# A Fourier mix and channel-mix kernel: the first two key pieces ordered by feature half, slots 4 to 7 mixed in four operations, one evacuation moved ahead of two

## The chip, the core and the metric

The kernel runs on one core of a Trainium2 chip. A core has a matrix engine (PE, with its weight loads shown apart as PEld), a vector engine (DVE), a scalar engine (ACT), a general engine (POOL) and a queue engine (SP). Each takes its own instructions in the order in which they were written, and engines wait for one another through semaphores. The metric is the time of one execution on the device in microseconds (us), lower is better; the median of several runs stands for a kernel.

## What is computed

For `x` of shape (8, 3072, 256): a two-dimensional Fourier transform per batch element, of which the real part is kept, and then a channel mix with a shift by one position.

```python
X = np.fft.fft(np.fft.fft(x, axis=1), axis=2).real       # (8, 3072, 256)
x_prev = X shifted by one position, zeros first
xk = mu_k * X + (1 - mu_k) * x_prev
xr = mu_r * X + (1 - mu_r) * x_prev
k = np.maximum(xk @ w_k, 0)                              # 256 -> 1024
v = (k * k) @ w_v                                        # 1024 -> 256
out = sigmoid(xr @ w_r) * v
```

`w_k` is (256, 1024), `w_v` (1024, 256), `w_r` (256, 256). The output is float32; inside, the kernel works in 16-bit floats with 32-bit sums.

## The kernel before

**Layout.** The transform is done as matmuls with tables of sines and cosines that the kernel builds at its start. Its result for a batch element is the tile `y` (in `y_t[b]`): 128 partitions hold features, the free axis holds slots of 64 positions, and in each slot the two feature halves `a = 0, 1` (features 0 to 127 and 128 to 255). Half of the sequence is covered by some 26 slots, and the other half is read from the mirrored ones. The mixed input `x` (`x_t[b, j, m]`; j = 0 for the key, 1 for the gate, m = 0 or 1 for the half of the sequence) has 24 slots for each feature half, that is 2 by 1536 columns.

**Mixing.** `diff` forms `d`, the difference of neighbouring slots, in one vector operation. `mix_part` then forms `x = y + mu * d` for a range of slots in one of two ways. For `j` = 0 and `lo` up to 4 it does one fused operation for each feature half (L738: multiply by a per-partition scalar, then add, in one instruction). Otherwise it does four operations: `scaled` for both halves (L711, a multiplication into the tile `t`), then `mixed` for both halves (L722, an addition). `mix_part` is called for the slots 4 to 7 and 8 to 15 of the first key input; the slots 0 to 3 have code of their own (L887 on ACT, then four fused operations on DVE, L892, two for each feature half), which takes them from PSUM.

**Key products.** The positions are worked in 48 chunks of 512 (`chunks`, each `(b, m, i)`), and each chunk in four K pieces (`ds` = 0 to 3). A piece gives 256 of the 1024 columns of `xk @ w_k` in a PSUM tile of 1024 columns from the three slots of `ps_w`. `k_products` (L749 to L760) issues its matmuls: two blocks of 128 columns (`hs`), and for each the two feature halves `a` = 0 and 1, which add up in PSUM; each matmul has a weight load of its own. `k_piece` issues the products, then the ReLU on ACT (L767). `square` squares the result on DVE (L777), or in a few steps on ACT (L775). `v_part` (L804) multiplies the squares by `w_v` in the first chunks, one piece at a time, three steps behind (`SHORT`); `v_tile` does so later on, a block of 128 positions at a time. `v_out` multiplies by the gate and sends the result out.

**Order.** The order of the instructions on every engine is the order in which the code issues them, which `pin_order` fixes at the end. The main loop runs over steps, one K piece each, and other work is hung on steps with `at` and `event`. Only the first chunk is special: its pieces 0 and 1 are done in two parts. The products for its first 256 positions (slots 0 to 3) are issued ahead of the main loop (L948, L949), those for its second 256 positions (slots 4 to 7) at steps 0 and 1.

**Around the change.** Ahead of the main loop the code issues, in this order: the two early products (L948, L949); `diff(0, 4, 8)` and `mix_part(0, 0, 4, 8)` on DVE; `d_small(0, 8, 2)` and `d_small(0, 10, 2)`, each four matmuls (L604) into one of the two PSUM slots of `ps_v` and an evacuation into `g_all` on ACT (L521); `y_evac(0, 0, 4, first)`, an evacuation of four slots of `y` on ACT out of the PSUM tile `first` (L521); then `diff(0, 8, 16)`. At step 0 follow `mix_part(0, 0, 8, 16)` and `diff(0, 0, 4)`, at step 1 one more `d_small`. The PSUM tile of piece 2 is the slot that `first` holds until then, and that of piece 3 is the slot of piece 0.

Of the kernel before, what the change touches and what calls it, by code (L numbers as in the profile page):

```python
# [20 lines left out]
def _v(ap, extra_offset, free_dims):  # L21
    new_ap = [list(ap.ap[0])] + [[s, c] for (s, c) in free_dims]
    return dataclasses.replace(ap, offset=ap.offset + extra_offset, ap=new_ap)
# [16 lines left out]
def kernel(  # L40
# [37 lines left out]
    def ps_w():  # L78
        return ps_slot("W", 3, 1024)

    def ps_v():
        return ps_slot("V", 2, 512)
# [434 lines left out]
    def evac(out_ap, in_ap, eng):  # L517
        if eng == "V":
            V.tensor_copy(out=out_ap, in_=in_ap)
        else:  # L520
            nc.scalar.activation(out=out_ap, in_=in_ap, func=AF.Copy)  # L521
# [75 lines left out]
    def d_units(b, ps, u0, n, bank):  # L597

        for i in range(n):
            for e in range(2):
                o = bank * e + 128 * i
                nc.tensor.matmul(out=ps[:, o:o + 128],  # L604
                                 lhsT=a_t[b][:, e, 2 * (u0 + i):2 * (u0 + i) + 2, :],
                                 rhs=w_eo[:, e], start=True, stop=True)

    def d_evac(ps, u0, n, bank, eng):
        evac(_v(g_all, 256 * u0, [(64, 2), (128, 2 * n), (1, 64)]),
             _v(ps, 0, [(bank, 2), (64, 2 * n), (1, 64)]), eng)  # L610
# [8 lines left out]
    def d_small(b, u, n, eng="A"):  # L619
        ps = ps_v()  # L620
        d_units(b, ps, u, n, 256)
        d_evac(ps, u, n, 256, eng)
# [35 lines left out]
    def y_evac(b, s0, n, ps):  # L658
        o = s0 % 2
        evac(y_t[b][:, s0:s0 + n].rearrange("p s a t -> p (s a t)"),  # L660
             _v(ps, 512 * o, [(128, n // 2), (512 - 1024 * o, 2), (1, 128)]), "A")
# [32 lines left out]
    def diff(b, lo, hi, hs=(0, 1)):  # L694
        if b not in x_t:
            x_t[b] = mix_pool.tile([P, 26, 2, 64], FP16, name="d")
        y = y_t[b]
        a0, a1 = hs[0], hs[-1] + 1
        V.tensor_tensor(out=x_t[b][:, lo:hi, a0:a1], in0=y[:, lo + 1:hi + 1, a0:a1],  # L699
                        in1=y[:, lo:hi, a0:a1], op=ALU.subtract)  # L700

    def scaled(b, j, m, a, lo, hi, eng="V"):

        if a == 0:
            x_t["t", a] = mix_pool.tile([P, 24, 64], FP16, name="t0")
        else:
            x_t["t", a] = mix_pool.tile([P, 24, 64], FP16, name="t1")
        mu = (mu_m if m else mu_f)[:, a, j:j + 1]
        src, dst = x_t[b][:, 2 * m + lo:2 * m + hi, a], x_t["t", a][:, lo:hi]
        if eng == "V":  # L710
            V.tensor_scalar(out=dst, in0=src, scalar1=mu, scalar2=None, op0=ALU.mult)  # L711
        else:
            nc.scalar.activation(out=dst, in_=src, func=AF.Copy, scale=mu)

    def mixed(b, j, m, a, lo, hi):

        if (a, lo) == (0, 0):
            x_t[b, j, m] = mix_pool.tile([P, 2, 1536], FP16, name=f"x{j}{m}")  # L720
        o, step = (1536 * a + 1535 - 64 * lo, -1) if m else (1536 * a + 64 * lo, 1)
        V.tensor_tensor(out=_v(x_t[b, j, m], o, [(64 * step, hi - lo), (step, 64)]),  # L722
                        in0=y_t[b][:, lo + 3 * m:hi + 3 * m, a], in1=x_t["t", a][:, lo:hi],
                        op=ALU.subtract if m else ALU.add)

    def mix_part(b, j, lo, hi):
        if j or lo > 4:
            for a in range(2):
                scaled(b, j, 0, a, lo, hi)
            for a in range(2):  # L730
                mixed(b, j, 0, a, lo, hi)
            return


        if lo == 0:
            x_t[b, j, 0] = mix_pool.tile([P, 2, 1536], FP16, name=f"x{j}0")
        for a in range(2):
            V.scalar_tensor_tensor(out=_v(x_t[b, j, 0], 1536 * a + 64 * lo,  # L738
                                          [(64, hi - lo), (1, 64)]),
                                   in0=x_t[b][:, lo:hi, a], scalar=mu_f[:, a, j:j + 1],  # L740
                                   in1=y_t[b][:, lo:hi, a], op0=ALU.mult, op1=ALU.add)
# [4 lines left out]

    k2_t, st = {}, {}

    def k_products(c, ds, lo=0, hi=512):  # L749
        b, m, i = c  # L750
        xk = x_t[b, 0, m]
        if lo == 0:
            st["k", ds] = ps_w()
        for hs in range(2):
            fc = 2 * ds + hs
            for a in range(2):
                nc.tensor.matmul(out=st["k", ds][:, 512 * hs + lo:512 * hs + hi],  # L757
                                 lhsT=wk_sb[m][a][:, 128 * fc:128 * fc + 128],
                                 rhs=xk[:, a, 512 * i + lo:512 * i + hi],
                                 start=(a == 0), stop=(a == 1))  # L760

    def k_piece(c, ds):
        if ds == 0:
            k2_t[c] = k2_pool.tile([P, 8, 512], FP16, name="k2", tag="k2")
            st["rl"] = k2_pool.tile([P, 8, 512], FP16, name="rl", tag="rl")
        k_products(c, ds, 256 if c == chunks[0] and ds < 2 else 0)
        nc.scalar.activation(out=st["rl"][:, 2 * ds:2 * ds + 2],  # L767
                             in_=st["k", ds].rearrange("p (f t) -> p f t", f=2),
                             func=AF.Relu, bias=0.0, scale=0.25)
# [101 lines left out]
    w, first = ps_w(), ps_w()  # L871
# [56 lines left out]
    chunks = [(b, m, i) for b in range(B) for m in range(2) for i in range(3)]  # L928
# [16 lines left out]
    for n, c in enumerate(chunks[:EARLY]):  # L945
        o_steps[4 * n + SHORT + 3] = [(c, 1, 2), (c, 3, 2)]
    o_steps[4 * EARLY + SHORT + 3] = [(chunks[EARLY], 1, 2)]
    k_products(chunks[0], 0, 0, 256)  # L948
    k_products(chunks[0], 1, 0, 256)  # L949
    diff(0, 4, 8)  # L950
    mix_part(0, 0, 4, 8)
    d_small(0, 8, 2)
    d_small(0, 10, 2)
    y_evac(0, 0, 4, first)
    diff(0, 8, 16)
    at(0, mix_part, 0, 0, 8, 16)
    at(0, diff, 0, 0, 4)
    at(1, d_small, 0, 12, 1)
    at(2, mix_part, 0, 1, 0, 8)
    event(3, (half_tables,))  # L960
    event(4, (c_item, 0, 17, 8))
# [67 lines left out]
    for b in range(B):  # L1029
# [9 lines left out]
        if t < B:  # L1039
# [6 lines left out]
            c = [(c_pairs, t, 8 * n, (8, 8, 8, 4)[n], EV[n]) for n in range(4)]  # L1046
# [21 lines left out]
    for step in range(nk + LAG):  # L1068
        if step < nk:
            k_piece(chunks[step // 4], step % 4)  # L1070
        due(step, "x")
        v = v_steps.get(step)
        if v and step not in early_v:
            v_tile(*v)
        if step in p_steps:
            v_part(*p_steps[step])
        due(step, "e")
        if step + 1 in early_v:
            v_tile(*v_steps[step + 1])
        early = step in OUT_FIRST  # L1080
        for v in o_steps.get(step, ()) if early else ():
            v_out(*v)
        due(step, "w")
        for v in () if early else o_steps.get(step, ()):
            v_out(*v)
        if step < 4 * EARLY + 4:
            square(chunks[step // 4], step % 4, 1, step in SQUARE_A)
        elif step < nk and step % 2:
            square(chunks[step // 4], step % 4)
# [32 lines left out]
```

## Time and profile before

| | |
|---|---|
| median of 3 runs | 431.68 us (431.59 to 433.62) |
| the profiled execution | 431.61 us, of which its span is 429.8 us |
| instructions in the span | 9301 |
| DMA traffic in the span | 42.06 MB, mean 98 GB/s |
| costliest group on PE | L757, the key products: 776 matmuls, 195.7 us busy |
| costliest group on ACT | L767, the ReLU: 192 instructions, 195.2 us busy |
| costliest group on DVE | L777, the squares: 101 instructions, 116.3 us busy |

All times of the profile are counted from the start of the span, and the execution's own time is 1.81 us longer than the span. In a timeline each row gives the start, the busy time, the engine, the line, the operation with output and inputs, the shape and the count; the bracket at the end gives idle time just before and what ended it. Rows of one operation can overlap a little, since an engine starts the next instruction while the last one drains. Ends of matmuls are modelled.

### The profile page before, as it was taken

The page shows a single profiled execution, that of the slowest core. Times are in us where ns is not written, and L with a number is a line of the kernel's source. Part 1 is how long each engine was busy: PE and PEld are TensorE (multiplying, and loading weights), DVE is VectorE, ACT ScalarE, POOL GpSimd, SP SyncE. Part 2 cuts the span into 40 slices and gives each one's busy share as a digit, 9 for nine tenths or more (in the row PEclk, how much of TensorE's full clock was granted, in tenths as well). Part 3 has the DMA queues.
Part 4 walks back from the last instruction along what each step waited for, and adds up shares of the span by engine and source line. Part 5 has one row for each costly group of instructions (what it writes and reads, how often), then busy time and mean ns, then how long its engine had stood idle before and what let it go on. Part 6 is the DMA issues. An engine that isn't in the chain of part 4 may idle for free.

```text
span 429.8 us, 9301 instructions
## 1 busy us (share of the span) xinstructions
PE 422.9 (98%) x3858; PEld 298.0 (69%) x3858; DVE 360.9 (84%) x547; ACT 320.2 (74%) x373; POOL 63.4 (15%) x96
## 2 busy tenths in 40 slices
PE   8999999999999999999999999999999999999996
PEld 3667776777777776776677777777767767766765
DVE  8899989997998889988898988989799847997453
ACT  7889897877878678776777777777786767666661
POOL 7686302000050002300041000500000000000000
PEclk9999999999999999999999999999999999999999
DMA  8999917322286233933269223763232322223233
GB/s 169 134 152 207 231 48 129 76 56 68 71 147 150 51 76 63 191 93 72 58 115 188 57 55 72 135 157 75 53 72 50 76 64 61 70 64 72 67 74 98
DMA packets 35103, 42.06 MB, mean 98 GB/s; under 512 B 4115, under 2 KB 31093, under 8 KB 35061
## 3 DMA queue, kind: packets, MB, share of 16 engines
q1 hardware_dynamic: 27488, 25.41, 23.7%
q0 software_dynamic: 7264, 15.80, 22.5%
q8 instruction: 30, 0.49, 0.5%
q10 hardware_dynamic: 308, 0.26, 0.2%
q14 instruction: 13, 0.10, 0.1%
HBM read 32.08 MB, written 25.17 MB: 133 GB/s over the span
## 4 chain that ended last, share of the span: by engine, by line
PE 94%; ACT 3%; DVE 1%; DMA 1%; issue 0%; ACTq 0%
PE psW L757 39%; PE psV L798 36%; PE psW L784 10%; PE psV L810 3%; PE psW L604 2%; PE psW L678 1%; PE psW L564 1%; DMA mu_row<-in_moe_mu_r_dram 1%; PE psW L646 1%; ACT a L521 1%; ACT m_cs L440 0%; PE psW L582 0%; ACT L839 0%; DVE x L892 0%; ACT rl L396 0%; ACT rl L767 0%
## 5 line engine op out<-in xcount | busy, mean ns | idle before, releaser
L767 ACT ACTIVATE rl<-psW 128x1024 f16<-128x1024 f32 x192 | 195.2, 1025 | 92.5 <-PE psW L757 89.0
L757 PE MATMUL psW<-x,wk 128*128 128x512 f16 (+1 forms) x776 | 195.7, 377 | 0.5
L798 PE MATMUL psV<-wv_sb,k 128*128 128x256 f16 x1424 | 184.1, 273 | 0.0
L798 PEld LDWEIGHTS <-k 128*128 128x128 f16 x1424 | 136.8, 98 | 35.9
L777 DVE TENSOR_TENSOR k<-rl 128x2048 f16<-128x2048 f16 (+1 forms) x101 | 116.3, 1152 | 33.4 <-ACT rl L767 33.0
L757 PEld LDWEIGHTS <-wk 128*128 128x128 f16 x776 | 74.8, 98 | 53.5 <-issue 1.3
L820 DVE SCALAR_TENSOR_TENSOR o<-psV,r 128x512 f32<-128x512 f32 (+1 forms) x97 | 65.8, 681 | 15.1 <-PE psV L798 13.5
L722 DVE TENSOR_TENSOR x<-y,t 128x1536 f16<-128x1536 f16 (+2 forms) x72 | 61.6, 860 | 2.1
L784 PE MATMUL psW<-wr,x 128*128 128x256 f16 x384 | 49.8, 273 | 0.0
L789 ACT ACTIVATE r<-psW 128x1024 f16<-128x1024 f32 x48 | 48.9, 1019 | 0.8 <-PE psW L784 0.8
L784 PEld LDWEIGHTS <-x 128*128 128x128 f16 x384 | 37.4, 98 | 14.4 <-issue 0.2
L463 POOL IOTA gate<- 1x1 int32 x6 | 2.1, 356 | 199.4 <-DVE gate L462 199.4
L521 ACT ACTIVATE a<-psW 128x832 f16<-128x832 f32 x31 | 25.9, 862 | 1.4 <-PE psW L564 1.4
L521 ACT ACTIVATE g_all<-psW 128x1024 f16<-128x1024 f32 (+5 forms) x37 | 25.6, 695 | 0.4 <-PE psW L627 0.2
L140 POOL DMA_INDIRECT xm<-in_x_dram,idx_g x18 | 24.2, 1344 | 5.5 <-issue 5.5
L171 DVE TENSOR_TENSOR p<-xp,xm 112x2304 f16<-112x2304 f16 (+6 forms) x19 | 21.6, 1139 | 0.0
L711 DVE TENSOR_SCALAR t<-d,muf_t 128x1536 f16<-128x1536 f16 (+2 forms) x40 | 20.8, 529 | 0.0
L711 DVE TENSOR_SCALAR t<-d,mu_m 128x1536 f16<-128x1536 f16 x32 | 19.6, 614 | 0.0
L604 PEld LDWEIGHTS <-a 128*128 128x128 f16 x208 | 14.0, 98 | 6.6 <-ACT a L521 0.6
L182 DVE TENSOR_TENSOR eo<-p 112x1152 f16<-112x1152 f16 (+3 forms) x28 | 17.9, 679 | 0.0
L521 ACT ACTIVATE pq<-psW 128x1024 f16<-128x1024 f32 (+1 forms) x18 | 15.2, 879 | 2.3 <-PE psW L678 2.3
L699 DVE TENSOR_TENSOR d<-y 128x1664 f16<-128x1664 f16 (+5 forms) x19 | 16.7, 880 | 0.0
(137 smaller groups left out, 217.7 us busy)
## 6 DMA issues: line engine op xcount, KB each, us to landing
out_dram<-o SPq DMA_DIRECT2D x189, 128.0 KB, 2.4
xp<-in_x_dram POOLq DMA_DIRECT2D x12, 216.0 KB, 4.5
xp<-in_x_dram POOLq DMA_DIRECT2D x13, 192.0 KB, 7.4
xp<-in_x_dram POOLq DMA_DIRECT2D x2, 384.0 KB, 6.9
wv_sb<-in_moe_w_v_dram POOLq DMA_DIRECT2D x1, 512.0 KB, 8.2
xp<-in_x_dram SPq DMA_DIRECT2D x1, 480.0 KB, 4.7
xp<-in_x_dram POOLq DMA_DIRECT2D x1, 432.0 KB, 6.4
xm<-in_x_dram,idx_g POOLq DMA_INDIRECT x18, 7.9
```

The source lines that it names most:

```text
L140: nc.gpsimd.indirect_dma_start(dst, None, src, bass.IndirectOffsetOnAxis(ap=idx, axis=0))
L521: nc.scalar.activation(out=out_ap, in_=in_ap, func=AF.Copy)
L604: nc.tensor.matmul(out=ps[:, o:o + 128], lhsT=a_t[b][:, e, 2 * (u0 + i):2 * (u0 + i) + 2, :], rhs=w_eo[:, e], start=True, stop=True)
L711: V.tensor_scalar(out=dst, in0=src, scalar1=mu, scalar2=None, op0=ALU.mult)
L722: V.tensor_tensor(out=_v(x_t[b, j, m], o, [(64 * step, hi - lo), (step, 64)]), in0=y_t[b][:, lo + 3 * m:hi + 3 * m, a], in1=x_t["t", a][:, ...
L757: nc.tensor.matmul(out=st["k", ds][:, 512 * hs + lo:512 * hs + hi], lhsT=wk_sb[m][a][:, 128 * fc:128 * fc + 128], rhs=xk[:, a, 512 * i + l ...
L767: nc.scalar.activation(out=st["rl"][:, 2 * ds:2 * ds + 2], in_=st["k", ds].rearrange("p (f t) -> p f t", f=2), func=AF.Relu, bias=0.0, sca ...
L777: V.tensor_tensor(out=k2_t[c][:, lo:hi], in0=r, in1=r, op=ALU.mult)
L784: nc.tensor.matmul(out=ps[:, 256 * tb:256 * tb + 256], lhsT=x_t[b, 1, m][:, a, 512 * i + 128 * tb: 512 * i + 128 * tb + 128], rhs=wr_sb[m] ...
L789: nc.scalar.activation(out=st["r", c], in_=ps, func=AF.Sigmoid)
L798: nc.tensor.matmul(out=st["v", tb - h][:, 256 * h:256 * h + 256], lhsT=k2_t[c][:, fc, 128 * tb:128 * tb + 128], rhs=wv_sb[:, fc], start=(f ...
L820: V.scalar_tensor_tensor(out=o.rearrange("p a b -> p (a b)")[:, 0:256 * n], in0=st["v", t0][:, 0:256 * n], scalar=16.0, in1=st["r", c][:, ...
```

## The change

Three things are edited. First, `k_products` takes the feature halves that it is to issue, and a new function, `k_early`, issues the products of pieces 0 and 1 of the first chunk in a given order of (feature half, piece): ahead of the loop first half of the features for both pieces, then the second half for both; in the loop the same, with the last group issued at step 1, behind the ReLU of piece 0 in the code. Second, `mix_part` uses the fused form for slots from 0 on alone, and so slots 4 to 7 of the first key input are mixed in four operations, not two. Third, `y_evac(0, 0, 4, first)` is issued ahead of the two `d_small`.

```diff
     def mix_part(b, j, lo, hi):
-        if j or lo > 4:
+        if j or lo:
             for a in range(2):
                 scaled(b, j, 0, a, lo, hi)
             for a in range(2):
...
-    def k_products(c, ds, lo=0, hi=512):
+    def k_products(c, ds, lo=0, hi=512, halves=(0, 1)):
         b, m, i = c
         xk = x_t[b, 0, m]
-        if lo == 0:
+        if lo == 0 and halves[0] == 0:
             st["k", ds] = ps_w()
         for hs in range(2):
             fc = 2 * ds + hs
-            for a in range(2):
+            for a in halves:
                 nc.tensor.matmul(out=st["k", ds][:, 512 * hs + lo:512 * hs + hi],
...
+    def k_early(lo, hi, which):
+        for a, ds in which:
+            k_products(chunks[0], ds, lo, hi, (a,))
+
     def k_piece(c, ds):
...
-        k_products(c, ds, 256 if c == chunks[0] and ds < 2 else 0)
+        if c == chunks[0] and ds < 2:
+            if ds == 0:
+                k_early(256, 512, ((0, 0), (0, 1), (1, 0)))
+            else:
+                k_early(256, 512, ((1, 1),))
+        else:
+            k_products(c, ds)
         nc.scalar.activation(out=st["rl"][:, 2 * ds:2 * ds + 2],
...
-    k_products(chunks[0], 0, 0, 256)
-    k_products(chunks[0], 1, 0, 256)
+    k_early(0, 256, ((0, 0), (0, 1), (1, 0), (1, 1)))
     diff(0, 4, 8)
     mix_part(0, 0, 4, 8)
+    y_evac(0, 0, 4, first)
     d_small(0, 8, 2)
     d_small(0, 10, 2)
-    y_evac(0, 0, 4, first)
     diff(0, 8, 16)
     at(0, mix_part, 0, 0, 8, 16)
     at(0, diff, 0, 0, 4)
```

## The prediction

> **What bounds the kernel now.** I read the page's span and engines first, then busy time by stretches, then the chain of waits.
>
> ```profile
> span 429.8 us, 9301 instructions
> PE 422.9 (98%) x3858; PEld 298.0 (69%) x3858; DVE 360.9 (84%) x547; ACT 320.2 (74%) x373; POOL 63.4 (15%) x96
> ```
>
> PE is busy for nearly the whole span. The stretches show where it is not; the columns are the stretch, its length, and the busy time and count for each engine, then the granted PE clock and the DMA share.
>
> ```profile
> 8.00:10.00 2.00, 1.44 (x10) 0.68 (x9) 1.97 (x4) 2.00 (x4) 1.68 (x7) 1.00 1.07 201
> 18.00:20.00 2.00, 1.80 (x24) 1.32 (x19) 1.97 (x6) 1.26 (x4) 1.39 (x2) 1.00 1.38 140
> 20.00:22.00 2.00, 1.86 (x13) 1.22 (x13) 1.96 (x6) 2.00 (x4) 1.70 (x2) 1.00 1.02 189
> 22.00:24.00 2.00, 1.99 (x13) 1.00 (x12) 2.00 (x5) 2.00 (x4) 1.62 (x6) 1.00 1.10 180
> ...
> 100.00:200.00 100.00, 100.00 (x934) 70.98 (x927) 88.43 (x114) 75.72 (x83) 12.84 (x16) 1.00 0.47 100
> ```
>
> From 100 to 200 us PE has no hole. The edits all lie between 17 and 24 us, where PE lacks 0.20, 0.14 and 0.01 us in three stretches. So whatever this change does is settled by the moment at which PE starts its unbroken run, and moves the end by as much. The chain of waits (start, length, what) names that moment:
>
> ```profile
> 17.38 1.13 DVE x L892 x4
> ...
> 19.47 0.89 DVE x L738 x2
> ...
> 20.41 0.93 PE psW L757 x7
> ...
> 21.44 1.87 PE psW L757 x8
> ...
> 23.32 1.05 PE psV L810 x8
> ```
>
> The chain runs on DVE to 20.36, through the pair L738 that the change splits, and then on PE. But a chain follows one releaser only. DVE itself, row by row, and the wait for its square:
>
> ```profile
> 18.42 0.68 DVE L519 CAST y<-psV 128x512 f16<-128x512 f32 x1
> 19.02 0.42 DVE L699 TENSOR_TENSOR d<-y 128x512 f16<-128x512 f16 x1
> 19.47 0.88 DVE L738 SCALAR_TENSOR_TENSOR x<-d,muf_t,y 128x256 f16<-128x256 f16 x2
> 20.27 0.69 DVE L699 TENSOR_TENSOR d<-y 128x1024 f16<-128x1024 f16 x1
> 20.99 0.67 DVE L711 TENSOR_SCALAR t<-d,muf_t 128x512 f16<-128x512 f16 x2
> 21.58 0.75 DVE L722 TENSOR_TENSOR x<-y,t 128x512 f16<-128x512 f16 x2
> 22.25 0.41 DVE L699 TENSOR_TENSOR d<-y 128x512 f16<-128x512 f16 x1
> 22.59 1.29 DVE L777 TENSOR_TENSOR k<-rl 128x1024 f16<-128x1024 f16 x2
> ...
> PEld L810 <- DVE k L777: 0.5, 1, 0.5
> ```
>
> The vector queue has no hole from 17.38 to the first two squares, 22.59 to 23.88, and L810, the first product with `w_v`, waits for the first square: its weight load stood 0.5 us. The first of the pair ends at about 22.59 + 0.67 = 23.26 (half of 1.29 and the drain), and L810 starts at 23.32. By the chain's modelled ends PE came from its key products at 21.44 + 1.87 = 23.31, so it was there just before. **Two conditions meet at 23.3: PE's own work and the vector queue.** A gain on PE alone shortens nothing, as the square does not move with it; a loss on DVE passes straight through.
>
> **Part 1, the order of the products.** Nothing is added: 16 matmuls of 256 columns before and after, with their weight loads.
>
> ```profile
> 18.15 1.34 PE L757 MATMUL psW<-x,wk 128*128 128x256 f16 x8
> 18.56 0.71 PE L757 MATMUL psW<-x,wk 128*128 128x256 f16 x5
> 19.32 0.61 PE L604 MATMUL psV<-w_eo,a 128*128 128x128 f16 x8
> ...
> 21.17 0.27 PE L604 MATMUL psV<-w_eo,a 128*128 128x128 f16 x2
> 21.37 1.94 PE L757 MATMUL psW<-x,wk 128*128 128x512 f16 x8
> ```
>
> The first matmul starts at 18.15, the second, which needs the other feature half, at 18.56, when L892 has ended at 18.51. From 18.56 to 19.32 seven go by, 0.108 us each. In the new order four of the first half run from 18.15 to 18.58, when the second half is ready, and all eight are through at 19.01, 0.31 us sooner. The eight L604 behind them need their two PSUM slots: DVE frees one at 18.42 + 0.68 = 19.10, ACT the other at 19.30 (first ACT row below), so they run from about 19.15 to 19.6, and not from 19.32 on, and the rest of the gain becomes a longer wait for slots 4 to 7.
>
> **Part 2, four operations for two.** The two L738 hold the queue from 19.47 to 20.27, 0.80 us start to start. No row shows a scaling of 256 columns; the nearest are these groups (busy, mean ns) and single rows:
>
> ```profile
> L711 DVE TENSOR_SCALAR t<-d,muf_t 128x512 f16<-128x512 f16 x10 | 3.1, 349 | 0.0
> L711 DVE TENSOR_SCALAR t<-d,mu_m 128x1536 f16<-128x1536 f16 x4 | 2.4, 612 | 0.0
> L265 DVE TENSOR_SCALAR w_pm<-w_pm 128x156 f16<-128x156 f16 x1 | 0.2, 201 | 0.0
> 29.98 0.60 DVE L711 TENSOR_SCALAR t<-d,muf_t 128x512 f16<-128x512 f16 x2
> 30.51 0.74 DVE L722 TENSOR_TENSOR x<-y,t 128x512 f16<-128x512 f16 x2
> 20.99 0.40 DVE L711 TENSOR_SCALAR t<-d,muf_t 128x512 f16<-128x512 f16 x1
> ```
>
> Scalings: two of 512 columns took 30.51 - 29.98 = 0.53 us start to start. From 1536 to 512 columns the duration falls by (612 - 349) / 1024 = 0.26 ns a column, so 256 fewer take 0.066 off each: 0.53 - 0.13 = 0.40 for the pair. Additions: 22.25 - 21.58 = 0.67 for two of 512; the same operation, as L699 in the rows of DVE, took 0.69 for 1024 columns and 0.41 for 512, 0.28 / 512 = 0.55 ns a column, 0.14 off each: 0.39. Together 0.79, **as much as the fused pair**. Bounds: from the 156-column row, 201 + 100 x (349 - 201) / 356 = 243 ns in place of 349 - 66 = 283, so 0.04 off each scaling, -0.08 at the low end. At the high end stands the 20.99 row: 0.40 us, where the group's mean is 0.349, and the pair took 21.58 - 20.99 = 0.59, 0.06 more than the quiet pair. POOL began an indirect DMA issue in the midst of that scaling, and it begins one in the midst of the new scaling too:
>
> ```profile
> 19.59 1.17 POOL L140 DMA_INDIRECT xm<-in_x_dram,idx  x1 [0.30 <-issue]
> 21.07 0.96 POOL L140 DMA_INDIRECT wr<-in_moe_w_r_dram,row_i  x1 [0.30 <-issue]
> 34.59 1.66 POOL L140 DMA_INDIRECT xm<-in_x_dram,idx_g  x1 [0.30 <-issue]
> 34.78 0.61 DVE L711 TENSOR_SCALAR t<-d,mu_m 128x1536 f16<-128x1536 f16 x1
> ```
>
> Of -0.08, 0 and +0.06 (+0.12 if both scalings are met) I take **+0.06**, since the 20.99 row is the nearest in time and in company. The added results come at 19.47 + 0.46 + 0.28 = 20.21 for the first half and 20.41 for the second, against 19.95 and 20.36 before; the first half is later, but part 1 puts four of its matmuls in a row. They run from 20.25 to 20.68, the other four to 21.11, L604 to 21.22. Before, the L604 pair began at 21.17, so PE is 0.06 ahead.
>
> **Part 3, the evacuation.** ACT's rows:
>
> ```profile
> 18.71 0.59 ACT L521 ACTIVATE y<-psV 128x512 f16<-128x512 f32 x1
> 19.75 1.09 ACT L521 ACTIVATE g_all<-psV 128x512 f16<-128x512 f32 x2 [0.44 <-PE psV L604]
> 20.71 0.60 ACT L521 ACTIVATE y<-psW 128x512 f16<-128x512 f32 x1
> 21.19 1.96 ACT L767 ACTIVATE rl<-psW 128x1024 f16<-128x1024 f32 x2
> ```
>
> ACT idles 0.44 us at 19.3, and the `y` evacuation, 0.60 us, moves into that hole: 19.30 to 19.90. Its PSUM slot, which piece 2 takes over (21.37, just behind the old end at 21.31), is free 1.4 us sooner, so piece 2 starts at 21.22, 0.15 earlier. Queued behind it, the two `g_all` evacuations run from about 19.8 to 20.9 as before, and the ReLU of piece 0 starts when its matmuls end, near 20.95, 0.24 earlier. None of this is on DVE. The cover of piece 1's late last group is ACT, busy with the first ReLU to about 21.95.
>
> **The sum.** PE arrives at L810 about 0.15 us sooner and waits there; the ReLU has ended by 22.0, well ahead of 22.6; the square comes with the vector queue, 0.06 later. Span 429.80 + 0.06 = 429.86, the profiled run 431.61 + 0.06 = 431.67, and the same on the median: 431.68 + 0.06, **431.7 us**. A measurement of this kernel can tell about 0.5% (2.16 us) from no change.
>
> **The rivals.** *PE's gain goes through.* If L810 is really held by PE, as the chain has it, and the scalings take the low bound, PE's 0.15 to 0.2 come off: 431.5. For it: the chain steps from 20.41 to 23.32 on PE. Against: the square ended within 0.06 of the start of L810, and DVE's queue has no hole to give. The ceiling is PE's idle time from 18 to 24 us, 0.20 + 0.14 + 0.01 = 0.35, so 431.3.
>
> *Slower: a scaling is shut out by POOL.* The second scaling, due at 19.74, falls wholly inside POOL's issue from 19.59 to 20.76. If it had to wait for that to end, DVE, the square and L810 would slip by 20.76 - 19.74 = 1.0 us: 432.7. It decides only if the wait lasts for the instruction. Against: the scaling at 34.78 ran inside POOL's issue from 34.59 to 36.25 and took 0.61, its group's mean. [...]
>
> *Slower: the moved evacuation waits for the mix.* If the write of slots 0 to 3 of `y` were held until the additions have read slots 4 to 7 (20.41), ACT would follow at its old spacing, 0.96 for the two `g_all` and 0.48 for itself: ReLU from 21.9 to 22.9. Piece 3 takes piece 0's slot then and ends near 23.8, L810 with it, 0.45 late: 432.1. Against: `d` at 19.02 read `y` while ACT's evacuation of other slots ran from 18.71 to 19.30, so regions are told apart.
>
> *Slower: PE's clock.* PE's waits gather into one of some 0.55 us, from 19.65 to 20.25. If the clock fell to half, the 2.9 us of work from 20.41 to 23.32 would take twice: 434.6. Against: from 8 to 10 us PE idled for 0.56 of 2.00, and the granted clock stayed at 1.00. [...]
>
> **How the numbers follow.** Forecast 0.73 (its own range 431.6 to 431.9), PE's gain through 0.11, shut out by POOL 0.05, evacuation held 0.05, clock 0.02, and 0.04 for the scatter of runs (one of the three shown lay at 433.62). The range takes in all but the last two: low 431.3 less the 0.1 by which the two close runs differ, 431.2; high 432.7 plus 0.1, 432.8. Beyond 2.16 us lie only the clock and the scatter, split evenly: slower 0.04, faster 0.02, same 0.94.
>
> **What would show it.** Right: the four vector operations take 0.8 to 0.9 us, the first square starts within 0.1 of 22.6, and the wait of L810 for it is longer than PE's whole gain. Wrong: L810 starts before 23.2; a scaling lasts over 0.5 us; the `y` evacuation starts after 20 us; the granted clock falls below 1.00; or the end moves although L810 did not, which would mean that something behind 24 us decides.

## The result, and the profile after

| | before | changed |
|---|---|---|
| median of four runs | 431.63 us (431.56 to 433.62) | 434.22 us (432.30 to 435.07) |
| ratio | | 1.0042, 95% interval 1.0022 to 1.0063 |
| the profiled execution | 431.61 us, span 429.8 | 432.30 us, span 430.5 |

The changed kernel came out slower, by 0.4% in the ratio, and its median lies 1.4 us above the upper end of the predicted range. Three of its four runs had a granted clock of 0.994 to 0.996 and lie at 433.8 to 435.1; executions at such a clock occur in the kernel before too and are some 1.4 us longer, so that the 432.30 of the profiled run, at 0.999, is the one to read for the change itself.

The page of the changed kernel, first lines:

```profile
span 430.5 us, 9303 instructions
PE 422.7 (98%) x3858; PEld 298.5 (69%) x3858; DVE 360.9 (84%) x549; ACT 320.3 (74%) x373; POOL 62.8 (15%) x96
```

Two more vector instructions, the same busy time on the vector engine (360.9), and a span that is 0.7 us longer. Busy time by stretches, columns as before:

```profile
18.00:20.00 2.00, 1.82 (x24) 1.38 (x21) 1.97 (x8) 1.70 (x5) 1.39 (x3) 1.00 1.30 148
20.00:22.00 2.00, 1.74 (x14) 1.28 (x14) 1.96 (x8) 1.09 (x3) 1.58 (x2) 1.00 1.06 179
22.00:24.00 2.00, 1.34 (x8) 0.58 (x6) 1.54 (x4) 2.00 (x3) 1.62 (x6) 1.00 1.07 152
```

PE stands idle for 0.66 us from 22 to 24 (busy for 1.34 of 2.00, where it had 1.99), and ACT, which had no hole from 20 to 22, has 1.09 of 2.00 there. The timeline's rows of the changed kernel, vector rows first, then ACT, then PE:

```profile
19.52 0.48 DVE L711 TENSOR_SCALAR t<-d,muf_t 128x256 f16<-128x256 f16 x2
19.92 0.48 DVE L722 TENSOR_TENSOR x<-y,t 128x256 f16<-128x256 f16 x2
20.33 0.68 DVE L699 TENSOR_TENSOR d<-y 128x1024 f16<-128x1024 f16 x1
22.91 0.69 DVE L788 TENSOR_TENSOR k<-rl 128x1024 f16<-128x1024 f16 x1 [0.24 <-issue]
19.25 0.60 ACT L521 ACTIVATE y<-psW 128x512 f16<-128x512 f32 x1
19.72 1.23 ACT L521 ACTIVATE g_all<-psV 128x512 f16<-128x512 f32 x2
21.85 1.94 ACT L778 ACTIVATE rl<-psW 128x1024 f16<-128x1024 f32 x2 [0.90 <-PE psV L604]
18.20 1.05 PE L757 MATMUL psW<-x,wk 128*128 128x256 f16 x8
20.26 1.03 PE L757 MATMUL psW<-x,wk 128*128 128x256 f16 x8 [0.44 <-DVE t L711]
21.24 1.03 PE L757 MATMUL psW<-x,wk 128*128 128x512 f16 x4
22.92 1.02 PE L757 MATMUL psW<-x,wk 128*128 128x512 f16 x4 [0.66 <-issue]
23.78 0.60 PE L821 MATMUL psV<-wv_sb,k 128*128 128x256 f16 x4
```

The three edits do what the prediction has them do: the order puts eight early matmuls in a row from 18.20, the four operations take 20.33 - 19.52 = 0.81 us, and the evacuation of `y` sits at 19.25. What does not fit is the ReLU of piece 0 (L778, which was L767). Its last matmul ends at about 21.07 by the modelled ends, and the ReLU starts at 21.85, after ACT has stood for 0.90 us. The first square (L788, which was L777) follows at 22.91, piece 3 waits for its PSUM slot, and the first product with `w_v` (L821, which was L810) starts at 23.78 in place of 23.32. So the first question was whether this late ReLU belongs to the change.

### The profile page after: what moved, and what is told of

Read it like the earlier page. It is cut to its first block, busy times and chain, and to the rows that moved or that the text cites. A ratio compares the mean times of both kernels' runs of the same rounds, so it can differ in the third digit from the quotient of the medians.

```text
span 430.5 us, 9303 instructions
## 1 busy us (share of the span) xinstructions
PE 422.7 (98%) x3858; PEld 298.5 (69%) x3858; DVE 360.9 (84%) x549; ACT 320.3 (74%) x373; POOL 62.8 (15%) x96
## 4 chain that ended last, share of the span: by engine, by line
PE 94%; ACT 3%; DMA 1%; DVE 1%; issue 0%; ACTq 0%
PE psW L757 39%; PE psV L809 36%; PE psW L795 10%; PE psV L821 3%; PE psW L604 2%; PE psW L678 1%; PE psW L564 1%; DMA mu_row<-in_moe_mu_r_dram 1%; PE psW L646 1%; ACT a L521 1%; ACT m_cs L440 0%; PE psW L582 0%; ACT L850 0%; DVE x L903 0%; ACT rl L396 0%
## 5 line engine op out<-in xcount | busy, mean ns | idle before, releaser
L778 ACT ACTIVATE rl<-psW 128x1024 f16<-128x1024 f32 x192 | 195.3, 1024 | 93.0 <-PE psW L757 88.6
L757 PE MATMUL psW<-x,wk 128*128 128x512 f16 (+1 forms) x776 | 195.4, 377 | 1.3 <-issue 0.7
L788 DVE TENSOR_TENSOR k<-rl 128x2048 f16<-128x2048 f16 (+1 forms) x101 | 116.4, 1152 | 33.9 <-ACT rl L778 33.0
L757 PEld LDWEIGHTS <-wk 128*128 128x128 f16 x776 | 74.9, 98 | 54.1 <-issue 2.0
L722 DVE TENSOR_TENSOR x<-y,t 128x1536 f16<-128x1536 f16 (+3 forms) x74 | 62.1, 845 | 2.1
L711 DVE TENSOR_SCALAR t<-d,muf_t 128x1536 f16<-128x1536 f16 (+3 forms) x42 | 21.2, 516 | 0.1
```

Source lines behind the costliest of these rows:

```text
L778: nc.scalar.activation(out=st["rl"][:, 2 * ds:2 * ds + 2], in_=st["k", ds].rearrange("p (f t) -> p f t", f=2), func=AF.Relu, bias=0.0, sca ...
L788: V.tensor_tensor(out=k2_t[c][:, lo:hi], in0=r, in1=r, op=ALU.mult)
```

## The experiments

They fell on four chips, called A to D here. Medians stand beside those of the kernel before on the same chip in the same set of runs: A 431.81 (35 runs), B 431.75 (29) and later 431.69 (25), C 431.67 (35, one of them at 1557.71), D 431.83 (29).

**The changed kernel again, and its three parts one by one (chip A).** `again` is the changed kernel without an edit.

> The changed kernel once more. Theory G (the matrix engine's clock: its waits now lie together, and in most executions the clock gate takes a stretch at half speed): executions spread from 432 to 435 us, and where the granted clock reads 0.994 to 0.996 the time is 1.5 to 2.5 us above an execution at 0.999. Theory R (the ReLU of piece 0 starts late, near 21.85 us and not 21.0, in every execution, whatever the clock): the ReLU starts after 21.7 us in this profile too, and the median stays above 432.2. Theory S (the first trace was an accident of that execution): ReLU near 21.0, first w_v product near 23.3, and 431.5 to 431.8 us.

`p1_order` has the order of the products alone, that is `k_products` with its halves, `k_early` and its calls.

> Only the order of the products of pieces 0 and 1; two fused operations for slots 4 to 7 and the evacuations as before. Theory G: the matrix engine finishes the early products 0.3 us sooner and then waits in one piece, so the lower clock shows in some executions and the median is 432.5 to 434.5. Theory R: the ReLU of piece 0 follows the evacuation at 21.2 as before, since ACT is busy until then; 431.6 to 432.0.

`p2_four` has the four operations alone:

```diff
-        if j or lo > 4:
+        if j or lo:
```

> Only the four operations in place of two for slots 4 to 7. Both theories: no wait is gathered and the vector queue is 0.06 us longer at most, so 431.6 to 431.8 us and a granted clock of 0.999 or more in all executions. If the four operations alone bring the lower clock or 432.5 us and more, both theories fall.

`p3_evac` has the early evacuation alone:

```diff
     mix_part(0, 0, 4, 8)
+    y_evac(0, 0, 4, first)
     d_small(0, 8, 2)
     d_small(0, 10, 2)
-    y_evac(0, 0, 4, first)
```

> Only the evacuation of y ahead of the two of g_all. Theory G: the matrix engine's waits stay as they were, 431.5 to 431.7. Theory R: if the late ReLU comes from the new order on ACT, it starts near 21.8 here too and the first w_v product after 23.7 (432.1 to 432.6); if not, it starts between 20.9 and 21.2 and the time is as before.

| chip A | median us | ratio, interval |
|---|---|---|
| again | 431.64 (11 runs) | 1.0002, 0.9986 to 1.0017 |
| p1_order | 431.87 (11) | 1.0002, 0.9989 to 1.0015 |
| p2_four | 431.67 (12) | 1.0004, 0.9988 to 1.0020 |
| p3_evac | 431.84 (11) | 1.0000, 0.9988 to 1.0011 |

Nothing moves the time here. The timeline of `again` follows the forecast, row by row, to about 0.1 us (vector, ACT, PE):

```profile
19.36 0.48 DVE L711 TENSOR_SCALAR t<-d,muf_t 128x256 f16<-128x256 f16 x2
20.16 0.68 DVE L699 TENSOR_TENSOR d<-y 128x1024 f16<-128x1024 f16 x1
20.88 0.62 DVE L711 TENSOR_SCALAR t<-d,muf_t 128x512 f16<-128x512 f16 x2
21.41 0.76 DVE L722 TENSOR_TENSOR x<-y,t 128x512 f16<-128x512 f16 x2
22.42 1.28 DVE L788 TENSOR_TENSOR k<-rl 128x1024 f16<-128x1024 f16 x2
25.45 0.25 DVE L503 CAST w_hh<-psW 112x104 f16<-112x104 f32 x1
30.21 0.60 DVE L711 TENSOR_SCALAR t<-d,muf_t 128x512 f16<-128x512 f16 x2
31.40 1.27 DVE L831 SCALAR_TENSOR_TENSOR o<-psV,r 128x512 f32<-128x512 f32 x2
19.08 0.60 ACT L521 ACTIVATE y<-psW 128x512 f16<-128x512 f32 x1
20.95 1.94 ACT L778 ACTIVATE rl<-psW 128x1024 f16<-128x1024 f32 x2 [0.28 <-PE psW L757]
23.04 1.96 ACT L778 ACTIVATE rl<-psW 128x1024 f16<-128x1024 f32 x2
24.84 0.24 ACT L521 ACTIVATE g_all<-psW 128x5 f16<-128x5 f32 x1
20.10 1.03 PE L757 MATMUL psW<-x,wk 128*128 128x256 f16 x8 [0.44 <-DVE x L722]
23.16 1.05 PE L821 MATMUL psV<-wv_sb,k 128*128 128x256 f16 x8
32.16 1.16 PE L821 MATMUL psV<-wv_sb,k 128*128 128x256 f16 x8
```

The ReLU starts at 20.95, as soon as its matmuls have ended, and L821 at 23.16. The whole trace lies some 0.1 us further left (its first L903, which was L892, at 17.27, in place of 17.38); from L903 to L821 go 5.89 us, and 5.94 went before. With the order alone L821 came at 23.18, with the four operations alone L810 at 23.32, with the early evacuation alone at 23.38; measured from their own first L903 or L892 that is 5.94, 5.89 and 5.93 us. So the late ReLU of the first trace is not a necessary part of the change.

**The changed kernel, a later ReLU, and a filled wait (chip B).** `again2` is the changed kernel without an edit.

> The changed kernel a third time, to see which of the first two measurements of it repeats. Theory G says that the change itself gathers the matrix engine's waits: its share of executions with a granted clock of 0.996 or less should be above that of the kernel before (10 of 35 in the last comparison, the changed kernel 4 of 11). Theory S (nothing of the first time comes from the change): share between 1 and 5 of 11, most executions within 0.2 us of the kernel before, median 431.5 to 432.0. If the first measurement repeats (all executions above 432.2), the result depends on the chip or on the loading, and S is too simple.

`late_relu` holds the ReLU of piece 0 back by a copy on ACT of 1280 columns that nobody reads, and prices a late ReLU by itself:

```diff
                 k_early(256, 512, ((0, 0), (0, 1), (1, 0)))
+                late = const.tile([P, 1280], FP16)
+                nc.scalar.activation(out=late, in_=y_t[c[0]][:, 0:10].rearrange("p s a t -> p (s a t)"),
+                                     func=AF.Copy)
```

> The changed kernel with a copy of 1280 columns on ACT ahead of the ReLU of piece 0 (it writes a tile that nobody reads), so that this ReLU starts about 0.8 us later, near 21.75 us, as it did at 21.85 in the first trace of the changed kernel. If the late ReLU is what made that trace longer, the chain is: ReLU ends 22.8, piece 3 (it takes piece 0's PSUM slot) starts 22.8 and ends 23.7, first w_v product 23.65 in place of 23.16: undisturbed executions 0.5 us above the changed kernel, 432.0 to 432.2. If instead the vector queue hides it, 431.6 to 431.8. Theory G adds: with a wait of 0.8 us more on the matrix engine the share of executions with a clock of 0.996 or less rises clearly above one in three, or the clock falls further.

`fill_gap` puts four products of zeros into the wait that the new order leaves on PE ahead of slots 4 to 7:

```diff
     d_small(0, 10, 2)
+    keep_busy(4, st["k", 1][:, 256:512], 256)
```

> The changed kernel with four matmuls of zeros, 256 columns each (0.43 us), into a part of PSUM that is overwritten, in the matrix engine's wait for slots 4 to 7 (19.66 to 20.10 in the last trace of the changed kernel). Theory G: the wait is what brings the half-speed stretch, so it is gone, no execution at 0.996, all within 431.4 to 432.1. If the stretch lies elsewhere, the share of executions at 0.996 stays near one in four and the time of the others is unchanged (the filled time is idle).

| chip B | median us | ratio, interval |
|---|---|---|
| again2 | 433.16 (12 runs) | 1.0026, 1.0016 to 1.0037 |
| late_relu | 432.49 (12) | 1.0012, 0.9999 to 1.0025 |
| fill_gap | 433.15 (12) | 1.0029, 1.0016 to 1.0041 |

Here the changed kernel is slower: eleven of its twelve executions lie at 433.03 to 433.45, at granted clocks of 0.998 to 1.0. The twelfth took 431.77, so the loss can stay away on this chip too. It is not the late ReLU of the first trace: in `again2` the ReLU of piece 0 starts at 20.98 and L821 at 23.19, and the time goes behind 24 us (rows below, from a second trace of the same kind). `fill_gap`, with PE's wait filled, does show the late ReLU again:

```profile
19.57 0.60 PE L206 MATMUL psW<-zeros 128*128 128x256 f16 x4
20.17 1.03 PE L757 MATMUL psW<-x,wk 128*128 128x256 f16 x8
...
21.76 1.94 ACT L778 ACTIVATE rl<-psW 128x1024 f16<-128x1024 f32 x2 [1.01 <-PE psV L604]
```

So the wait of PE ahead of slots 4 to 7 is not the cause of the late ReLU; ACT waits as long without it. This trace is of an execution at 432.22, one of the three fastest of `fill_gap`; no trace shows where the eight at 432.9 to 433.4 lose their time. `late_relu` is the surprise. Its rows, in a trace that lies 1.7 us further right at this place (a stretch of low clock, last section):

```profile
23.56 1.93 ACT L781 ACTIVATE rl<-psW 128x1024 f16<-128x1024 f32 x2
24.62 1.02 PE L757 MATMUL psW<-x,wk 128*128 128x512 f16 x4 [0.84 <-ACT rl L781]
```

The ReLU is late by design and PE waits 0.84 us for it; the price is about 0.7 us (the nine executions at clocks of 0.998 to 1.0 lie at 432.18 to 432.62), where 0.5 was expected. And that leaves it *below* the changed kernel, of which it contains every part. Whatever costs `again2` its 1.4 us does not strike when ACT's work lies some 0.9 us later (its ReLU of piece 0 starts 4.61 us behind the first L906, which was L903, and 3.68 in `again2`).

**The kernel before, and two of the parts, on the same chip (B).** `before_copy` is the kernel before without an edit, built anew; `again3` the changed kernel; `p1_order2` and `p2_four2` are as `p1_order` and `p2_four`.

> The kernel before, unchanged, built and loaded anew like a changed one. In the traces of the changed kernel that were 0.7 and 1.4 us longer (the first and the third), semaphore updates of the matrix engine are recorded 0.5 to 2.4 us after the matmul that makes them, and about 200 of the 4116 updates by DMAs are missing from the first 40 us; in the others all are there and on time. Theory C (the chip or the loading does that, to any kernel): this one shows it too where the changed kernel does, and its median is then 432.3 to 433.5. Theory K (only the changed order is met by it): 431.6 to 431.9 beside a changed kernel at 432.3 or more.

> The changed kernel a fourth time, beside the copy of the kernel before. Theory C: as the copy, whatever that is, within 0.3 us. Theory K: 432.3 to 433.5 with the late updates, while the copy stays at 431.7. If both are at 431.5 to 431.9, this chip doesn't show the late updates and the two theories stand as they are.

> Only the order of the products, once more. Under theory K with the order of the products as the part that matters (it makes the ReLU of piece 0 wait for PE's update instead of for ACT): late updates and 432.3 or more, where the changed kernel has them. Under theory C as the others of this call.

> Only the four operations, once more. It has the same two vector instructions more than the kernel before as the changed kernel has, and no other order on PE and ACT. If the number of instructions (where the program lies when loaded) is what matters: late updates and 432.3 or more, where the changed kernel has them. If the order on PE or ACT matters: 431.6 to 431.9.

| chip B | median us | ratio, interval |
|---|---|---|
| before_copy | 431.68 (12 runs) | 0.9999, 0.9990 to 1.0008 |
| again3 | 433.23 (7) | 1.0037, 1.0024 to 1.0051 |
| p1_order2 | 431.73 (12) | 1.0002, 0.9992 to 1.0012 |
| p2_four2 | 433.19 (8) | 1.0035, 1.0022 to 1.0048 |

On this chip the four operations alone cost as much as the whole change, and the order alone costs nothing (the early evacuation alone was not run on it). Where it goes, in the timeline of `again3` (ACT, vector, PE, POOL):

```profile
24.73 1.02 ACT L778 ACTIVATE rl<-psW 128x1024 f16<-128x1024 f32 x1 [0.52 <-PE psW L500]
27.02 0.19 ACT L521 ACTIVATE g_all<-psW 128x5 f16<-128x5 f32 x1 [1.26 <-remote]
27.24 0.27 DVE L503 CAST w_hh<-psW 112x104 f16<-112x104 f32 x1 [1.58 <-ACT g_all L521]
31.64 0.85 DVE L711 TENSOR_SCALAR t<-d,muf_t 128x512 f16<-128x512 f16 x2
33.08 1.27 DVE L831 SCALAR_TENSOR_TENSOR o<-psV,r 128x512 f32<-128x512 f32 x2
23.29 1.05 PE L821 MATMUL psV<-wv_sb,k 128*128 128x256 f16 x8
27.26 0.40 PE L646 MATMUL psW<-m_cs,g_all 64*128 64x128 f16 x8 [0.68 <-ACT g_all L521]
33.81 0.87 PE L821 MATMUL psV<-wv_sb,k 128*128 128x256 f16 x5 [0.51 <-DVE o L831]
31.64 0.70 POOL L420 MEMSET xp<- 32x256 f16 x2
```

Set these against the rows of `again` above. L821 starts at 23.29, 0.13 later, which is the shift of the whole trace (its first L903 is at 17.40). The small evacuation of `g_all` starts at 27.02 in place of 24.84, 2.18 late; PE's L646 needs it and stands 0.68 us; the vector engine's cast of `w_hh` (27.24 in place of 25.45) is 1.79 late. ("Remote" names no engine; the instruction on ACT just ahead of it waits for PE's semaphore.) **One event, two payments.** PE's own share is in at 27.26, where it is 0.97 behind. The vector queue carries its part on: it makes up little of it, is still 1.43 behind at 31.64 (30.21 before), and 1.68 behind at 33.08, where it takes the results of L821 out of PSUM. PE waits for that PSUM slot and pays the rest at 33.81, 1.65 behind 32.16. From there the distance stays about the same to the end (spans 431.5 and 429.7). The step from 1.43 to 1.68 is a collision of its own: the two scalings at 31.64 start together with POOL's memset and take 0.85 us, not 0.60.

The timeline of `p2_four2`, whose trace lies some 1.6 us further right (a stretch of low clock at 12 us, below), has the same rows behind 24 us (the first row belongs to the last section):

```profile
10.42 1.71 PE L582 MATMUL psW<-w_pm,p 96*128 96x208 f16 x16 [1.50 <-DVE p L173]
...
28.57 0.19 ACT L521 ACTIVATE g_all<-psW 128x5 f16<-128x5 f32 x1 [1.22 <-PE psW L757]
28.82 0.40 PE L646 MATMUL psW<-m_cs,g_all 64*128 64x128 f16 x8 [0.53 <-ACT g_all L521]
33.19 0.85 DVE L711 TENSOR_SCALAR t<-d,muf_t 128x512 f16<-128x512 f16 x2
35.36 1.19 PE L810 MATMUL psV<-wv_sb,k 128*128 128x256 f16 x8 [0.50 <-DVE o L820]
```

And the kernel before on the same chip (`before_copy`) has the evacuation on time:

```profile
23.28 1.99 ACT L767 ACTIVATE rl<-psW 128x1024 f16<-128x1024 f32 x2
25.09 0.27 ACT L521 ACTIVATE g_all<-psW 128x5 f16<-128x5 f32 x1
```

Why does ACT stand? The trace's record of PE's semaphore, which is all that those ACT instructions wait for, against the modelled end of the matmul that raises it (us; rises and matmuls are paired in order):

```
kernel (chip)      matmul          its end   raised   ACT starts
again (A)          L757, piece 3   23.05     23.06    23.94, behind the ReLU before
again (A)          L500            24.39     24.41    24.43
again3 (B)         L757, piece 3   23.18     24.71    24.73
again3 (B)         L500            24.52     26.93    26.96
changed, first     L757, piece 0   21.07     21.83    21.85
before_copy (B)    L604            21.41     21.74    22.11, behind the ReLU before
before_copy (B)    L500            24.52     24.53    24.55
p1_order2 (B)      L604            19.83     20.36    20.39
p1_order2 (B)      L646            27.00     27.31    27.33
before_copy (B)    L757            25.43     none     25.47
```

In `again3` and in the first trace of the changed kernel ACT starts 0.02 us behind the recorded rise, and the rise comes 0.75 to 2.4 us behind the matmul's end. In none of the traces of A, C and D, nor in that of the kernel before in front of the change, does a rise of this semaphore come more than 0.05 us behind its matmul. Chip B's records are also thin: where the traces of A, C and D hold 5772 to 5780 rises of all semaphores, those of B, the kernel before included, hold 5502 to 5542, and the first trace of the changed kernel 5538. That alone costs nothing: the last row shows a rise without a record, and ACT went on as if it had come.

Late rises are not confined to the four operations. Every trace of chip B has some, the kernel before and the order alone among them; but in `before_copy` they are 0.3 us late in the first 40 us and meet an ACT that is busy, and in `p1_order2` up to 0.66, of which ACT's wait for L646 pays some 0.3 (it stood 0.70 us ahead of 27.33, and 0.41 ahead of the same evacuation in `before_copy`). What differs on this chip is how late they are at 23 to 25 us, and whether ACT stands there for them.

**Is it the instructions or their number (chip C, then D)?** `rest_only` is the changed kernel with the fused operations for slots 4 to 7 again, so parts 1 and 3 alone. `tiny2` is the kernel before with two vector operations of 16 columns behind the fused pair, `tail2` the same with two of 2 columns at the very end; nobody reads their results. `again4` is the changed kernel.

```diff
     mix_part(0, 0, 4, 8)
+    tiny = const.tile([P, 2, 16], FP16)
+    for h in range(2):
+        V.tensor_scalar(out=tiny[:, h], in0=x_t[0][:, 4, h, 0:16], scalar1=mu_f[:, h, 0:1],
+                        scalar2=None, op0=ALU.mult)
```

> The changed kernel with slots 4 to 7 mixed in two fused operations again: the order of the products and the early y evacuation stay. Theory (the four operations alone bring the lost 1.4 to 1.55 us, behind 24 us): 431.7 us, 0.9990 to 1.0010 of the kernel before, where again4 of the same call gives 433.2. Rival (another part takes part in it): 432.5 or more beside again4 at 433.2. If again4 too stays at 431.7, this chip doesn't show the loss and the run settles nothing.

> The kernel before, with two vector operations of 16 columns on a tile that nobody reads added right behind the fused mixing of slots 4 to 7: the number and place of the vector instructions are those of the change, their work is not. Theory 1 (two more instructions in the vector queue at this place are enough): 433.2 us, with the two stalls at 24.6 to 27.3 and at 31.6 to 33.7 us, beside again4 at 433.2. Theory 2 (the work itself, that is what the four operations read, write or when they end, brings it): 431.7 to 431.9, of which 0.1 to 0.2 us is that the vector queue gives the first w_v product's inputs later.

> The kernel before with two vector operations of 2 columns at the very end of the program, on a tile that nobody reads: only the length of the vector queue's program is that of the changed kernel. Theory 1 (place decides) and theory 2 (the work decides): 431.7 us, as the kernel before. Rival (the mere length or layout of the program brings it): 433.2 us with the stalls at 24.6 to 27.3 and 31.6 to 33.7 us.

> The changed kernel once more, as the measure for the other three of the call: 433.2 us (1.003 of the kernel before) with the two stalls behind 24 us, if the chip is of the kind that showed them; 431.7 us without them, if it is of the other kind. Either bears on whether the loss belongs to the kernel alone or to kernel and chip together.

`again4` was at 431.65 (ratio 0.9996, 0.9983 to 1.0009), so chip C does not show the loss, and the other three (431.71, 431.88 and 431.70) can't tell. They were tried once more and fell on chip D:

> Parts 1 and 3 with the fused mixing, as rest_only. If again5 of this call gives 433.2 us: 431.7 by the theory that the four operations alone bring the loss; 432.5 or more by the rival that another part has a share in it. If again5 gives 431.7, this says nothing new.

> The kernel before with two vector operations of 16 columns behind the fused mixing, as tiny2. If again5 gives 433.2 us: 433.2 with the stalls at 24.6 to 27.3 and 31.6 to 33.7 us if two more vector instructions at this place are enough; 431.9 if the work of the four operations is needed. If again5 gives 431.7, this says nothing new.

> The changed kernel as the measure of this call: 433.2 us with the two stalls on a chip whose traces lack some 200 semaphore updates of the first 40 us, 431.7 on one whose traces have them all.

`again5` was at 431.60 (1.0000, 0.9988 to 1.0013), `rest_only2` at 431.97, `tiny3` at 432.00: nothing lost again. So what the loss on chip B needs, the work of the four operations or just two more instructions, wasn't settled.

## Why the prediction was wrong

**What bounds the kernel, up to 24 us: right.** Two conditions meet at the first product with `w_v`, and neither the order nor the evacuation moves it. On chip A it started within 0.05 us of where it was, measured from the first L903 or L892. `tiny2` and `tiny3`, which give the vector queue some more work and change nothing else, have L810 at 6.15 and 6.16 us behind the first L892, where it was 5.94, and medians 0.2 us above those of the kernel before; that fits "a loss on DVE passes straight through", though a step of that size alone is within the scatter.

**Part 1: right.** The early products are through 0.3 us sooner and the gain becomes a wait: 0.44 us ahead of 20.10 in `again`, where 0.55 was foreseen.

**Part 2: right in its size, not in its sign.** The four operations take 0.80 us in `again` and 0.81 in the first trace. The +0.06 that was taken for POOL's DMA issue did not show; the middle value, no difference, was the better choice for the pair itself. The whole moved the other way: L821 or L810 comes 5.89 us behind the first L903 or L892 in every trace with the four operations and an on-time ReLU, and 5.93 or 5.94 in those with the fused pair and nothing added. That 0.05 is found at the next pair of scalings, which takes 21.41 - 20.88 = 0.53 us in `again` and took 21.58 - 20.99 = 0.59. POOL's issue begins 0.08 us after that pair starts in the kernel before and 0.12 us ahead of it in `again`.

**Part 3: right.** The evacuation moved into ACT's hole (19.08), and the ReLU came at 20.95, as soon as its matmuls had ended; with the shift of the trace taken off that is 0.1 us behind the time foreseen.

**The sum: right on three of the four chips of the experiments**, 431.60 to 431.65 us, with intervals of the ratio that all hold 1. It missed on chip B and in the runs of the result. **The step that failed** is the one that closed the first part: "whatever this change does is settled by the moment at which PE starts its unbroken run, and moves the end by as much". On chip B L821 starts on time and the end moves by 1.4 to 1.5 us, since ACT gets PE's semaphore up to 2.4 us late at 24 to 27 us and the vector queue, as full there as it was ahead of 23 us, carries the delay on to 33.8 us. The prediction named this sign (an end that moves although L810 did not) and gave it no price. In the first trace of the changed kernel it is another step, "the ReLU of piece 0 starts when its matmuls end, near 20.95": it starts 0.78 us behind that end, and the span grows by 0.7.

**The rivals.** None of the four is what happened. No scaling was shut out by POOL's DMA issue (two, from 19.52, took 0.48 us in the first trace, overlap counted once, where POOL's issue ran from 19.65 to 20.62). The evacuation of `y` was not held by the mix; the ReLU at 21.85 looks like that rival's 21.9, but the evacuation had started at 19.25. The clock does fall in some executions, with the change and without it (means of 0.996 in most of these, 0.991 in the lowest); in the two traces that show it, it fell at 12.0 and 11.4 us, ahead of the change. PE's gain did not go through.

**The size.** The 2.59 us between the two medians of the result is not one effect: 0.7 us is the difference of the profiled executions, and the other three runs have the lower clock besides. What those three lost in which place no trace shows.

**What stays open.** That the late semaphore makes the loss is read from the rows; why PE's semaphore rises late on one chip and not on three others, and why by 0.3 to 0.7 us in the kernel before and the order alone and by up to 2.4 with the four operations, was not found. Every execution on record has a span and a granted clock of its own, so these runs can't tell either whether the recording, which is thin on this chip, holds the rises up itself: that rival is untested. `late_relu`, which holds every part of the change and loses less, and the one execution of `again2` at 431.77 speak for a matter of instants, and not of the work. Which chip the runs of the result used is not known; the thin record of the changed kernel's trace there (5538 rises) is like those of B, that of the kernel before (5773) like those of the other three, so the two profiles that the prediction and the result are read from may not be of one chip.

## What to carry to other kernels

An unbroken run of the bounding engine in one trace doesn't prove that nothing behind it decides: look also at whether the second engine (here the vector queue) has any hole in which a late start can be made good, and price a delay of a microsecond there. Before a change of a tenth of a per cent is believed in either direction, run the same kernel again on other chips, with the kernel before beside it: here one and the same kernel gave a ratio of 0.9996 on one and 1.0037 on another, with intervals that do not meet. A part that is neutral by every row of its own stage can still shift instants into a bad meeting further on, so its price is known only from the end of the program.

## What the runs showed of the hardware

**PE's semaphore came up to 2.4 us after the matmul.** At most 0.05 us in twelve traces, 0.1 to 2.4 us in some places in those of chip B and in the first trace of the changed kernel, in some of them with ACT standing idle for it. The rises of the vector engine's and ACT's own semaphores that are on record in these traces are none of them over 0.1 us late. The ends of matmuls are modelled, so the distance has some play, but not of 2 us: PE's next instructions start on time (L821 of `again3` at 23.29, 0.11 us behind the end of piece 3's L757).

**A memset on POOL and two scalings on the vector engine took longer together than apart.** In `again3` the pair of 512-column scalings took 0.85 us beside the memset, which took 0.70 for two; in `again` they took 0.60 and 0.55 apart. So there is a price, here 0.25 us, but it is not the whole length of the memset: the first of the two scalings took 0.45 us beside a memset of 0.30, and 0.33 by itself, so that a wait for the whole memset would have made it 0.64. The scaling of 1536 columns inside POOL's DMA issue (34.78 in the kernel before), at its usual 0.61, shows no price.

**In the two traces that show it, the half-speed stretch lies ahead of the change and has one length.** Eight of the 35 executions of the kernel before on chip A had a granted clock of 0.996 and took 433.06 to 433.46 us (the expectation of `again2` counts ten). Where it falls, by stretches of `p2_four2`, columns as before:

```profile
10.00:12.00 2.00, 1.58 (x17) 1.39 (x17) 1.90 (x8) 1.97 (x4) 1.54 (x4) 1.00 0.75 121
12.00:14.00 2.00, 2.00 (x13) 1.57 (x11) 1.32 (x5) 1.61 (x4) 1.77 (x5) 0.50 0.97 140
14.00:16.00 2.00, 2.00 (x13) 1.53 (x11) 1.17 (x3) 1.19 (x2) 1.38 (x3) 0.64 0.88 124
16.00:18.00 2.00, 1.94 (x30) 1.39 (x28) 1.14 (x5) 1.53 (x5) 0.00 (x0) 1.00 1.03 123
```

The clock is at half from 12.0 to 15.4 us, some 3.4 us: all 2.00 of the one stretch, and 1.44 of the next, which makes its mean 0.64. In `late_relu` it was half from 11.4 to 14.8, as long (the means of its stretches from 10, 12 and 14 us are 0.86, 0.50 and 0.79). PE stood 1.50 us ahead of L582 at 10.42 in `p2_four2` (row above) and 1.76 in `late_relu`.

The length of that wait hardly tells the two apart from the rest. In the eighteen traces at full clock PE stood 0.14 to 1.46 us at this place, 1.46 in `rest_only`, 0.04 less than in `p2_four2`. With two cases on the one side and so small a gap, it is not shown that the wait brings the fall, and no run here changed the wait by intent.
